# Query pass of linear attention mixed into the GLU stage, sigmoid by tanh, 1/den by head

## The chip, the core and the metric

The kernel runs on one core of one Trainium2 chip. The metric is the device time of one execution in microseconds (us).

Five engines work side by side, each through its own queue in order: TensorE (PE in the profile) multiplies matrices, VectorE (DVE) and ScalarE (ACT) do elementwise work, POOL (GpSimd) does a little of it and hands out most stores, SyncE (SP) hands out most loads and all transposing transfers.

## The reference, cut to what matters

Four residual layers, attention, GLU, attention, GLU, forward and backward in one launch. S = 2048 rows, D = 512, F = 1376, 32 heads of 16. Inputs and outputs are bf16.

```python
def _A_ref(x, wqkv, wo):                       # layers 0 and 2
    ...
    phi = lambda t: jnp.where(t > 0, t + 1, jnp.exp(t)) + 1e-6
    pq, pk = phi(q), phi(k)
    kv = jnp.einsum("bhsd,bhse->bhde", pk, v)
    z = jnp.einsum("bhsd->bhd", pk)
    num = jnp.einsum("bhqd,bhde->bhqe", pq, kv)
    den = jnp.einsum("bhqd,bhd->bhq", pq, z)[..., None] + 1e-6
    o = num / den
    return (... o ...) @ wo

def _B_ref(x, w_gate, w_up, w_down):           # layers 1 and 3
    g = jnp.einsum("bsd,df->bsf", x, w_gate)
    u = jnp.einsum("bsd,df->bsf", x, w_up)
    return jnp.einsum("bsf,fd->bsd", _sigmoid(g) * u, w_down)

x = x + _A_ref(_layernorm(x), A_wqkv, A_wo);  x = x + _B_ref(_layernorm(x), ...)   # twice
# outputs: x and, by jax.vjp, the gradients of x and of all weights
```

An attention layer has two passes. The first takes all keys into a sum (E and z). The second, the **query pass**, needs that sum: queries q, the map phi, the denominator den, the division, the output product y.

## The kernel before

The rows are cut into four blocks of 512 (SB). The parts that the change and the argument touch:

```python
def q_block(k, hT):                            # queries and phi of one block
    for d2 in range(NDC // 2):
        for dc in (2 * d2, 2 * d2 + 1):
            mm4(k, q_ps[:], ...)                                           # TensorE, 4 matmuls
            nc.scalar.activation(eq[:, dc, :], q_ps[:], ACT.Exp)
        nc.vector.tensor_scalar(e2, e2, 1.0, None, ALU.min)                # the clamp
        nc.vector.tensor_scalar(a_t[:], e2, EPS, None, ALU.add)
        for i, dc in ...:
            nc.vector.scalar_tensor_tensor(pq[:, dc, :], qs[i][:], 1.0 + EPS, a_t[:, i, :], ALU.add, ALU.max)
# ... the query pass, after the first pass is over:
    for b in range(NBLK):
        for dc in range(NDC):
            nc.tensor.matmul(d_ps[:], lhsT=Z[:, dc, :], rhs=pe[:, 0, dc, :], ...)   # den, for every channel
            nc.scalar.activation(ld[:], d_ps[:], ACT.Ln, bias=k.eps[:])
            nc.scalar.activation(rd[:], ld[:], ACT.Exp, scale=-1.0)                 # 1/den
            nc.vector.tensor_tensor(qr[:, :, dc, :], pe[:, :, dc, :], rd[:]..., ALU.mult)
        # store qr, turn it (qn) by a transposing transfer, store qn
        if b + 2 < NBLK: qb.append(q_block(k, ln.hT[b + 2]))
        if b: out(b - 1)                       # y of the block before, LayerNorm of the next layer
# ... a unit of the GLU, layers 1 and 3 (eleven a block):
    mm4(k, g_ps[:], ...); mm4(k, u_ps[:], ...)
    nc.scalar.activation(sd[:, 0, :], g_ps[:], ACT.Sigmoid)
    nc.scalar.activation(oms[:], g_ps[:], ACT.Sigmoid, scale=-1.0)
    nc.vector.tensor_tensor(hh[:], u_ps[:], sd[:, 0, :], ALU.mult)
    nc.gpsimd.tensor_tensor(sd[:, 1, :], hh[:], oms[:], ALU.mult)
    # layer 3 also: mm4(dhh_ps), nc.scalar.copy(dhh, ps), dd = dhh * sd on VectorE
```

Weights that layer 3 needs turned (wdT, wuT, wgT) come by transposing transfers on SyncE's queue.

## Time and profile before

1213.13 us, the median of three runs (1212.6 to 1213.26). The trace handed over with it, however, is of another clock. The first experiment profiled the unchanged kernel again, at the timed clock. Columns: span, mean granted clock.

The trace handed over with the kernel before:

```profile
core 0: 1450.6 us, clock 0.749
```

The same kernel profiled again (run e0_before):

```profile
core 0: 1214.3 us, clock 0.969
```

All numbers "before" from here on are of this second trace, except in the prediction, which had only the first.

### The profile page before, as it was taken

Reading aid. Unit: us, or ns where it says so; the run is one execution under the profiler, and the core shown is the slowest. Engines: PE = TensorE matmul, PEld = TensorE weight load, DVE = VectorE, ACT = ScalarE, POOL = GpSimd, SP = SyncE. Lnnn points to the kernel's source line nnn. Section 1 sums busy time; section 2 is a strip of 40 time slices with the busy share of each in tenths; the row PEclk is TensorE's granted clock in tenths of the full one; section 3 lists DMA queues with packets and bytes.
Section 4 is the critical chain, followed back from the end, with each engine's and each line's share of the span. In section 5 each row is a group of like instructions: output and inputs, shape, how many; then the busy total and the mean of one; then the engine's idle time right before and its main releaser. Section 6 shows DMA issues by size and latency. Waiting matters only on the chain.

```text
span 1450.6 us, 14906 instructions
## 1 busy us (share of the span) xinstructions
PE 1392.4 (96%) x5323; PEld 582.4 (40%) x5408; DVE 533.5 (37%) x976; ACT 477.0 (33%) x951; POOL 385.3 (27%) x496
## 2 busy tenths in 40 slices
PE   6989999998999999998999999998999999999997
PEld 3433333443343333333443333443333334533433
DVE  6584333477335243424665344465730000000000
ACT  5475443267514041515336233352440000000000
POOL 4117654104505040402444111143440000000100
PEclk8777777777777777777777777777777777777777
DMA  7978564659915041316847645469539554794651
GB/s 225 226 196 236 196 192 158 145 115 251 256 47 164 26 139 37 104 36 203 297 139 165 210 158 172 162 226 269 176 90 265 130 131 105 174 218 111 154 129 32
DMA packets 355786, 234.47 MB, mean 162 GB/s; under 512 B 279232, under 2 KB 332448, under 8 KB 351616
## 3 DMA queue, kind: packets, MB, share of 16 engines
q1 hardware_dynamic: 336144, 158.24, 44.5%
q0 software_dynamic: 19568, 75.28, 14.3%
q8 instruction: 42, 0.69, 0.2%
q14 instruction: 32, 0.26, 0.1%
HBM read 67.14 MB, written 97.81 MB: 114 GB/s over the span
## 4 chain that ended last, share of the span: by engine, by line
PE 73%; issue 15%; DVE 4%; DMA 4%; POOL 2%; ACT 1%; SPq 1%; another core or an unknown queue 0%; POOLq 0%; DVEq 0%; ACTq 0%
PE dw_ps L996 12%; PE y_ps L162 7%; PE dh_ps L632 7%; PE dh_ps L721 7%; PE g_ps L162 6%; PE u_ps L162 6%; PE dhh_ps L162 6%; PE dh_ps L932 4%; PE q_ps L162 2%; PE dpk_ps L162 2%; PE E_ps L414 2%; PE k_ps L162 2%; PE dh_ps L861 2%; PE dq_ps L162 2%; PE CT_ps L777 2%
## 5 line engine op out<-in xcount | busy, mean ns | idle before, releaser
L996 PE MATMUL dw_ps<-set_t,h_all 128*128 128x512 bf16 (+1 forms) x1008 | 266.6, 439 | 1.7 <-issue 0.2
L996 PEld LDWEIGHTS <-h_all 128*128 128x128 bf16 x1024 | 115.0, 112 | 153.0 <-issue 131.6
L959 ACT CAST dw_new<-dw_ps 128x512 bf16<-128x512 f32 (+2 forms) x51 | 25.2, 578 | 344.7 <-issue 244.0
L960 POOL DMA_DIRECT2D out_dram<-dw_new x51 | 27.4, 542 | 347.9 <-ACT dw_new L959 300.9
L162 PE MATMUL g_ps<-hT_t,wg 128*128 128x512 bf16 x352 | 116.5, 463 | 3.3 <-DMA hT_t<-h_t 2.3
L162 PE MATMUL u_ps<-hT_t,wu 128*128 128x512 bf16 x352 | 116.1, 464 | 0.0
L162 PE MATMUL dhh_ps<-gT_t,wdT 128*128 128x512 bf16 x341 | 113.2, 461 | 0.8
L1010 PE MATMUL dw_ps<-g_all,set_t 128*128 128x512 bf16 (+1 forms) x345 | 99.3, 463 | 0.7
L595 POOL TENSOR_TENSOR sd_t<-hh_t,oms 128x512 bf16<-128x512 bf16 x44 | 51.9, 1180 | 128.6 <-DVE hh_t L594 125.6
L721 PE MATMUL dh_ps<-wgT,dd_t 128*128 128x512 bf16 x174 | 80.4, 462 | 0.9
L721 PE MATMUL dh_ps<-wuT,dd_t 128*128 128x512 bf16 x167 | 77.1, 462 | 1.7 <-DVE dd_t L746 1.6
L162 PEld LDWEIGHTS <-wg 128*128 128x128 bf16 x352 | 39.7, 113 | 63.9 <-issue 63.8
L721 PEld LDWEIGHTS <-dd_t 128*128 128x128 bf16 x352 | 39.7, 113 | 62.0 <-issue 59.0
L1010 PEld LDWEIGHTS <-set_t 128*128 128x128 bf16 (+1 forms) x352 | 40.5, 115 | 59.2 <-issue 55.1
L162 PEld LDWEIGHTS <-wu 128*128 128x128 bf16 x352 | 39.8, 113 | 60.5 <-issue 60.5
L632 PEld LDWEIGHTS <-dd_t 128*128 128x128 bf16 x352 | 39.5, 112 | 60.3 <-issue 60.3
L162 PEld LDWEIGHTS <-wdT 128*128 128x128 bf16 x352 | 39.1, 111 | 60.5 <-issue 60.5
L746 DVE TENSOR_TENSOR dd_t<-dhh_t,sh_t 128x1024 bf16<-128x1024 bf16 x44 | 33.3, 758 | 81.9 <-ACT dhh_t L744 81.9
L785 POOL TENSOR_TENSOR dqT_t<-w_t,qr_l 128x512 bf16<-128x512 bf16 x32 | 38.3, 1208 | 77.3 <-DMA qr_l<-sv_qr_118 39.3
L685 ACT ACTIVATE t_sb<-dh_ps,rstd_132 128x512 f32<-128x512 f32 x16 | 11.0, 687 | 134.8 <-PE dh_ps L632 134.8
L536 POOL TENSOR_TENSOR sd_t<-hhT_t,oms 128x512 bf16<-128x512 bf16 x44 | 51.1, 1177 | 13.9 <-DVE hhT_t L535 9.7
L601 DVE TENSOR_TENSOR dd_t<-dhh_t,sd_t 128x1024 bf16<-128x1024 bf16 x44 | 32.2, 731 | 60.3 <-POOL sd_t L595 59.3
(542 smaller groups left out, 2132.6 us busy)
## 6 DMA issues: line engine op xcount, KB each, us to landing
sv_ddT_123<-dd_t SPq DMA_DIRECT2D x40, 256.0 KB, 2.2
sv_ddT_110<-dd_t SPq DMA_DIRECT2D x40, 256.0 KB, 2.8
sv_sd_112<-sd_t POOLq DMA_DIRECT2D x8, 1024.0 KB, 4.3
sh_t<-sv_sd_112 SPq DMA_DIRECT2D x8, 1024.0 KB, 6.0
out_dram<-dw_new POOLq DMA_DIRECT2D x42, 128.0 KB, 3.6
sv_hhT_109<-hhT_t POOLq DMA_DIRECT2D x4, 1280.0 KB, 6.5
sv_hhT_122<-hh_t POOLq DMA_DIRECT2D x40, 128.0 KB, 2.2
sv_qr_105<-qr_t POOLq DMA_DIRECT2D x4, 1024.0 KB, 5.9
```

Of the source, the lines that this page charges most:

```text
L162: i = k.nc.tensor.matmul(out, lhsT=lhs(c), rhs=rhs(c), start=(c == 0), stop=(c == n - 1))
L414: nc.tensor.matmul(E_ps[ic][:], lhsT=h[:, ic * P:(ic + 1) * P], rhs=pk, start=(st == 0), stop=(st == NST - 1))
L536: pooled(k, nc.gpsimd.tensor_tensor(sd[:, 1, i, :], hhT[:, fc, :], oms[:], ALU.mult))
L595: nc.gpsimd.tensor_tensor(sd[:, 1, :], hh[:], oms[:], ALU.mult)
L601: mul = nc.vector.tensor_tensor(dd[:], dhh[:].unsqueeze(1).to_broadcast([P, 2, SB]), sd[:], ALU.mult)
L632: k.nc.tensor.matmul(dh_ps[:], lhsT=dds[fc][:, a, rows(j)], rhs=(k.wuT, k.wgT)[a][:, fc, :], start=(i == 0), stop=(i == 2 * NFC - 1))
L721: nc.tensor.matmul(acc[b][j][:], lhsT=dd[:, a, rows(j)], rhs=(k.wuT, k.wgT)[a][:, fc, :], start=(fc == 0 and a == 0), stop=(fc == NFC - 1 ...
L746: nc.vector.tensor_tensor(dd[:], dhh[:].unsqueeze(1).to_broadcast([P, 2, SB]), sh[:, :, i, :], ALU.mult)
L785: nc.gpsimd.tensor_tensor(dqT[:, dc, :], w_t[:], rp[:, dc, :], ALU.mult)
L932: nc.tensor.matmul(dh[j][:], lhsT=lhs(j, c), rhs=rhs(c), start=False, stop=stop and c == NDC - 1)
L996: k.nc.tensor.matmul(ps[ic][:, 0:w], lhsT=h_t[:, ic * P:(ic + 1) * P], rhs=t, start=(i == 0 and st == 0), stop=(i == len(srcs) - 1 and st ...
L1010: k.nc.tensor.matmul(p[0:r, :], lhsT=t[:, f:f + r], rhs=g_t, start=(i == 0 and st == 0), stop=(i == len(srcs) - 1 and st == NST - 1))
```

## The change

Its intent: let TensorE do GLU matmuls while VectorE and ScalarE catch up with the query pass. For that the query pass becomes a generator that hands out small units, half of them before the GLU starts, half among its units. Mixing the two would switch ScalarE's function tables all the time, so sigmoid becomes 0.5(1 - tanh(-g/2)) out of the table that has exp. The Trainium skill ("ScalarE: Activation LUTs", Table sets: the hidden batching unit) lists exp and tanh in one set; the trace has four table loads before (1.28 us each). That table names ln only in another set, and run g2 below, which takes Ln and Exp back while keeping tanh, has five table loads. So 1/den is taken by head: 64 short matmuls, a reciprocal, a mask, and 16 matmuls that spread it over the channels. One clamp per pair goes to POOL.

```diff
@@ forward @@
-            a_fwd(k, 0, lns[0], lns[1])
-            b_fwd(k, 1, lns[1], lns[2])
+        second = A0.second(lns[1])
+        next(second)                                  # the half before the GLU
+        for b, fc in b_fwd(k, 1, lns[1], lns[2]):
+            next(second, None)                        # one unit after each GLU unit
+            if b == NBLK - 1 and fc in (4, 6, 8, 10):
+                A2.keys((fc - 4) // 2)
         ... the same for layers 2 and 3, two units per GLU unit of block 0;
         ... wuT and wgT are asked for when the query pass is used up (before: at units 0 and 4)
@@ query @@
-        nc.vector.tensor_scalar(e2, e2, 1.0, None, ALU.min)
-        nc.vector.tensor_scalar(a_t[:], e2, EPS, None, ALU.add)
+        nc.vector.tensor_scalar(a_t[:], pe[:, 1], 1.0, EPS, ALU.min, ALU.add)
+        nc.gpsimd.tensor_scalar(pe[:, 1], pe[:, 1], 1.0, None, ALU.min)
@@ den and share @@
-            nc.tensor.matmul(d_ps[:], lhsT=Z[:, dc, :], rhs=pe[:, 0, dc, :], ...)
-            nc.scalar.activation(ld[:], d_ps[:], ACT.Ln, bias=k.eps[:])
-            nc.scalar.activation(rd[:], ld[:], ACT.Exp, scale=-1.0)
+        for j in range(NB):
+            for dc in range(NDC):
+                nc.tensor.matmul(d_ps[32 * j:32 * j + 32, :], lhsT=self.Z[:, dc, :],
+                                 rhs=self.pe[b, dc // 2][:, 0, dc % 2, rows(j)], ...)
+        nc.scalar.activation(d_t[:], d_ps[:], ACT.Identity, bias=k.eps[:])
+        nc.vector.reciprocal(d_t[:], d_t[:])
+        nc.vector.tensor_tensor(self.RD[b][:], d_t[:]..., k.tmask[:]..., ALU.mult)
+            nc.tensor.matmul(ps[:], lhsT=k.spread[:, 2 * d2 + i, :], rhs=self.RD[b][:]..., ...)
+            nc.scalar.copy(rd[:, i, :], ps[:])
@@ second, layer 2 @@
+            k.wdT = k.p_wa.tile([P, NDC, F], BF16, name="wdT", tag="wkvo")   # in the place of wk, wv, wo
+            nc.sync.dma_start_transpose(out=k.wdT[:], in_=k.w_in["wd"])      # so only when these are used up
@@ glu @@
-    nc.scalar.activation(sd[:, 0, i, :], g_ps[:], ACT.Sigmoid)
-    nc.scalar.activation(oms[:], g_ps[:], ACT.Sigmoid, scale=-1.0)
+    nc.scalar.activation(th[:], g_ps[:], ACT.Tanh, scale=-0.5)
+    nc.scalar.activation(sd[:, 0, :], th[:], ACT.Identity, bias=k.onef[:], scale=-1.0)
+    nc.scalar.activation(sd[:, 1, :], th[:], ACT.Identity, bias=k.onef[:])
```

Cut from this diff: buffers (six shared ones for queries and keys in place of pools of two), saving MT and kv to memory for the backward, a few forced orders at the start, and wdT's reload in the backward.

## The prediction

> **What bounds it now.** The page's busy table has TensorE busy 1392 of 1450.6 us (96%); VectorE 37%, ScalarE 33%, POOL 27%. But this execution fell in a slow state: the clock record holds 0.752 from 25 us on with only one core running. The Trainium skill ("TensorE: Matmul & The Clock Gate", the limiter note in Part 1) says one or two busy cores never trip the limiter; this trace disagrees. The timed runs (1213 us) must have had a higher clock. The timeline shows back-to-back 512-column matmuls every 284 ns; by that page's N/2.4+2.5 they take 216 ns at full clock. About 4900 such matmuls (counted from the source) give an estimate of 1058 us, so in timed runs some 90 to 155 us are not TensorE: more than the 58 us idle shown here. What is TensorE-bound in the trace can be bound by the other engines when timed.
>
> **Where that idle time lies.** The table of 10 us stretches: in attention's second pass (60 to 110 us and 298 to 350 us) VectorE is busy 8 to 9 and ScalarE up to 9.5 of each 10 us. Per layer I sum VectorE at about 50 us (q 16 x 0.69, clamps 16 x 0.43, q/den 16 x 0.69, residual 16 x 0.69, LN, copies), ScalarE 34 to 40 (Exp 0.60, Ln 0.69, Exp(-ln) 0.63, copies 0.59), against TensorE 160 matmuls = 45 us here, 35 us at full clock. So about 15 us per attention layer are lost when timed. Smaller losses: start (11.5 us in the first 20); 2.6 us at 36 us (key pool of two, waiting on key transposes); 2.3 us before layer 3's first g (hidden state's transpose); 4.4 us at 662 us (chain: wqkv's transpose 6.8, then qr load 5.3).
>
> **What the change does.**
> - Half of each second pass runs among GLU matmuls, the rest before them: the prefix still has about 33 us of VectorE work against 25 us of TensorE. I expect 8 to 10 us back per layer.
> - Ln+Exp (1.31 us x 16 per layer) becomes a 0.59 us copy; three of four table loads (1.28 us each) go; one clamp per pair goes to POOL.
> - TensorE gains 16 spreading matmuls per layer and 64 short den matmuls for 16 long: 4 to 4.5 us per layer, on the critical path.
> - GLU on ScalarE: two sigmoids (1.19) become tanh and two affine passes (estimate 1.9 from the Ln and Exp forms). With the dhh copy that is 2.5 us per unit against 2.6 us of TensorE: nearly critical in layer 3, with slack in down and dh.
> - Six key/query buffers and keys taken early: 4 to 6 us. Instruction order: qr's load now precedes wqkv's transpose: 3 to 4 us.
> - Costs: wuT/wgT requested at the tenth unit instead of the first and fifth; they took 20 us in the trace, needed after about 17: 2 us. wdT's transpose (10.5 us) stands before layer 3's first hidden transposes: 0 to 5 us. MT reloaded: 1 us.
>
> **Sum:** about -33 + 9 = -24 us.
>
> Predicted 1189 us, 80% range 1168 to 1210. Chances: faster over 2% 0.50, same 0.46, slower 0.04.
>
> **Shown right if** the second pass has no stretches with TensorE below 9 of 10 once GLU matmuls start; only one table load remains; rd matmuls cost about 3.5 us per layer; layer 3's unit pitch stays at twelve matmuls. **Wrong if** ScalarE exceeds TensorE in the GLU units (TensorE waiting on a g or u bank), if the gap before layer 3's first g grows, or if dh waits for wuT.
>
> **What would make it wrong:** a timed clock below full, which shrinks the idle time to be won while the added matmuls stay; ScalarE's three passes being slower; POOL's clamp and VectorE holding each other up.

## More of the kernel before

The instruction groups of VectorE in layer 0's query pass (busy us, mean ns of one | idle time before them):

```profile
L336 DVE SCALAR_TENSOR_TENSOR pe_t<-q_ps,a_t 128x512 bf16<-128x512 f32 x16 | 10.4, 684 | 0.1
L473 DVE TENSOR_TENSOR qr_t<-pe_t,rd_t 128x1024 bf16<-128x1024 bf16 x15 | 10.0, 686 | 1.4 <-ACT rd_t L472 1.3
...
L334 DVE TENSOR_SCALAR a_t<-pe_t 128x1024 bf16<-128x1024 bf16 x8 | 3.6, 450 | 0.1
L333 DVE TENSOR_SCALAR pe_t<-pe_t 128x1024 bf16<-128x1024 bf16 x8 | 3.4, 421 | 0.8 <-ACT pe_t L329 0.8
```

L333 is the clamp: 0.42 us each, 3.4 us a layer. That is what the change moves to POOL.

The view by windows gives, for a stretch of time, its length and each engine's busy time (number of instructions in brackets). I chose four stretches: the two query passes alone (layers 0 and 2, each from the last matmul of the first pass to the first GLU matmul), and the query pass together with the GLU layer that follows (up to the last product with w_down for layers 0 and 1; up to the last forward matmul for layers 2 and 3).

```profile
core 0: us, PE busy (x) PEld busy (x) DVE busy (x) ACT busy (x) POOL busy (x), PEclk, DMA share, GB/s
55.90:98.70 42.80, 35.77 (x187) 15.80 (x184) 38.39 (x83) 34.02 (x61) 8.20 (x15) 0.96 0.84 214
260.20:306.30 46.10, 36.15 (x187) 15.88 (x184) 40.67 (x89) 36.98 (x68) 8.77 (x16) 0.96 0.74 188
...
55.90:224.90 169.00, 156.26 (x731) 69.16 (x727) 99.57 (x198) 102.07 (x203) 96.18 (x131) 0.98 0.76 229
260.20:547.80 287.60, 269.68 (x1251) 120.62 (x1248) 152.33 (x273) 133.50 (x267) 102.57 (x137) 0.98 0.54 145
```

Read it so: in layer 0's query pass TensorE works 35.8 of 42.8 us and is idle 7.0; in layer 2's it is idle 10.0. So 17 us is all of TensorE's idle time that there is to win in the two query passes. VectorE is busy 38.4 of the 42.8 us (90%): it is nearer its limit than TensorE (84%), and POOL is nearly free. In the longer stretches TensorE is idle 12.7 and 17.9 us.

TensorE's timeline shows where it waits: the bracket at a line's end is the idle time just before it and what ended it. Three of its waits in layer 3 and at the start of the backward:

```profile
306.33 0.59 PE L162 MATMUL g_ps<-hT_t,wg 128*128 128x512 bf16 x1 [3.03 <-DMA hT_t<-h_t]
...
346.45 1.86 PE L162 MATMUL g_ps<-hT_t,wg 128*128 128x512 bf16 x4 [7.92 <-DVE hh_t L594]
...
563.63 0.61 PE L782 MATMUL t_ps<-u_t,bdmask 128*128 128x512 bf16 x1 [7.62 <-DVE u_t L817]
```

The last two have nothing to do with the query pass.

## The result, and the profile after

The changed kernel is right and takes 1244.98 us, the median of four runs (1242.17 to 1248.96); the kernel before in the same rounds took 1213.2 (1212.6 to 1213.55). The ratio is 1.0265, 95% interval 1.0236 to 1.0294: slower by 2.65%, where I had predicted 1189 us, faster. Ratios here and below are the mean time of one kernel's fast runs over that of the other's of the same rounds, so not quite the ratio of the medians that are quoted.

The two traces, cut at the last forward matmul: the forward grew from 547.8 to 578.1 us (+30.3), the backward shrank by 4.1. The same two long stretches as before, by windows:

```profile
core 0: us, PE busy (x) PEld busy (x) DVE busy (x) ACT busy (x) POOL busy (x), PEclk, DMA share, GB/s
56.30:243.20 186.90, 164.23 (x806) 72.25 (x803) 111.43 (x200) 124.38 (x238) 134.39 (x169) 0.95 0.75 214
272.50:578.10 305.60, 272.32 (x1319) 122.07 (x1316) 157.29 (x269) 153.95 (x303) 128.68 (x151) 0.96 0.54 146
```

TensorE's idle time in them was to go. It grew, from 12.7 to 22.7 us and from 17.9 to 33.3 us. Its busy time grew too, by 8.0 and 2.6 us (some of that are keys of layer 2 that are now taken in layer 1). VectorE, which was to be relieved, has 11.9 and 5.0 us more; POOL has 38 and 26 us more.

TensorE's timeline has four large waits that the kernel before does not have:

```profile
130.03 1.86 PE L179 MATMUL u_ps<-hT_t,wu 128*128 128x512 bf16 x4 [6.83 <-ACT rd_t L475]
...
313.95 0.26 PE L458 MATMUL den_ps<-pe_t,Z_t 128*32 128x128 bf16 x1 [11.50 <-DVE pe_t L450]
322.50 0.61 PE L179 MATMUL g_ps<-hT_t,wg 128*128 128x512 bf16 x1 [8.29 <-DMA hT_t<-h_t]
...
394.60 1.86 PE L704 MATMUL dh_ps<-wgT,sd_t 128*128 128x512 bf16 x4 [4.57 <-DMA wgT<-in_B_w_gate_dram]
```

The second and third answer to the 3.03 us wait before (layer 3's first GLU matmul). Follow them back. POOL's timeline just before:

```profile
296.03 0.23 POOL L255 TENSOR_SCALAR ln_neg<-x_sum 128x2 f32<-128x2 f32 x1
306.23 0.64 POOL L379 DMA_DIRECT2D sv_qn_125<-qn_t  x1 [9.97 <-DMA qn_t<-pe_t]
306.95 0.18 POOL L261 TENSOR_SCALAR rstd_140<-ln_ss 128x2 f32<-128x2 f32 x1
```

POOL stood for 10 us at a store (of the turned queries, qn) whose data had not landed, and LayerNorm's tiny rstd stood behind it. The SyncE queue tells why the data was late: wdT's transpose takes 8.8 us of the queue, then the two transposes of qn 5.7, and the last hidden state (hT) that the GLU needs comes after the gradient's transpose of 5.7 us.

```profile
289.64 8.83 SPq L557 DMA_TRANSPOSE wdT<-in_B_w_down_dram  x1
298.52 5.73 SPq L480 DMA_TRANSPOSE qn_t<-pe_t  x2
...
308.86 5.70 SPq L644 DMA_TRANSPOSE gT_t<-in_grad_out_dram  x1
314.66 2.03 SPq L266 DMA_TRANSPOSE hT_t<-h_t  x1
```

VectorE, in order too, waits 7.7 us for that rstd, with the residual and the next queries behind it:

```profile
308.72 1.28 DVE L264 TENSOR_SCALAR h_t<-x_90,ln_neg,rstd_140 128x512 bf16<-128x512 f32 x1 [7.68 <-POOL rstd_140 L262]
```

The wait at 130 us has the same form: POOL's in-order queue of clamps (2.8 us each), products and stores delays ln_neg, ScalarE stands at the LayerNorm instruction behind it, and 1/den's copy (rd) stands behind that:

```profile
126.76 0.72 ACT L259 ACTIVATE ln_junk<-x_96,ln_neg 128x512 bf16<-128x512 f32 x1 [7.25 <-POOL ln_neg L255]
```

The Trainium skill ("PSUM — Partial Sum Buffer", Engine vs sequencer instructions) says that the queues of ScalarE, VectorE and GpSimd (POOL) "are strict FIFO"; these lines are what that looks like when two stages share them.

Last, the GLU's three ScalarE passes, whole program (before: two Sigmoids of 0.60 us each, 1.19 us a unit):

```profile
L602 ACT ACTIVATE sd_t<-th_t,onef 128x512 bf16<-128x512 f32 x88 | 63.4, 721 | 3.2
L604 ACT ACTIVATE sd_t<-th_t,onef 128x512 bf16<-128x512 f32 x88 | 62.3, 708 | 0.0
L601 ACT ACTIVATE th_t<-g_ps 128x512 f32<-128x512 f32 x88 | 51.3, 587 | 15.6 <-PE g_ps L179 14.8
```

2.02 us a unit, near the 1.9 that I had estimated.

After this reading I had two theories: Q, three waits behind queues (behind wdT's transpose, behind the clamp on POOL, behind wuT and wgT) are the loss; S, ScalarE's third pass is. Later runs forced a third, V: the new 1/den and the clamp on POOL cost what they cost, whether mixed or not.

### The profile page after: what moved, and what is told of

It reads as the page before. It is cut to its first block, busy times and chain, and to the rows that moved or that the text cites. A ratio compares the mean times of both kernels' runs of the same rounds, so it can differ in the third digit from the quotient of the medians.

```text
span 1240.5 us, 15505 instructions
## 1 busy us (share of the span) xinstructions
PE 1109.0 (89%) x5536; PEld 511.5 (41%) x5536; DVE 548.4 (44%) x968; ACT 513.2 (41%) x1020; POOL 454.0 (37%) x563
## 5 line engine op out<-in xcount | busy, mean ns | idle before, releaser
L1070 PE MATMUL dw_ps<-set_t,h_all 128*128 128x512 bf16 (+1 forms) x1024 | 207.3, 366 | 3.1 <-DMA set_t<-sv_ddT_116 3.1
L1070 PEld LDWEIGHTS <-h_all 128*128 128x128 bf16 x1024 | 100.9, 99 | 109.3 <-issue 7.2
L605 POOL TENSOR_TENSOR sd_t<-sd_t,hh_t 128x512 bf16<-128x512 bf16 x88 | 105.6, 1200 | 105.5 <-ACT sd_t L604 45.0
L179 PE MATMUL g_ps<-hT_t,wg 128*128 128x512 bf16 x352 | 93.6, 389 | 12.3 <-DMA hT_t<-h_t 11.5
L179 PE MATMUL u_ps<-hT_t,wu 128*128 128x512 bf16 x352 | 92.8, 387 | 7.7 <-ACT rd_t L475 7.4
L179 PE MATMUL dhh_ps<-gT_t,wdT 128*128 128x512 bf16 x352 | 89.8, 379 | 0.0
L179 PE MATMUL y_ps<-wd,hh_t 128*128 128x512 bf16 x352 | 78.0, 379 | 2.0 <-DVE hh_t L603 2.0
L603 DVE SCALAR_TENSOR_TENSOR hh_t<-sd_t,u_ps 128x512 bf16<-128x512 bf16 x88 | 60.1, 683 | 25.3 <-ACT sd_t L602 23.4
L602 ACT ACTIVATE sd_t<-th_t,onef 128x512 bf16<-128x512 f32 x88 | 63.4, 721 | 3.2
L604 ACT ACTIVATE sd_t<-th_t,onef 128x512 bf16<-128x512 f32 x88 | 62.3, 708 | 0.0
L601 ACT ACTIVATE th_t<-g_ps 128x512 f32<-128x512 f32 x88 | 51.3, 587 | 15.6 <-PE g_ps L179 14.8
L676 DVE TENSOR_TENSOR sd_t<-dhh_t,sd_t 128x1024 bf16<-128x1024 bf16 x44 | 33.4, 761 | 51.1 <-POOL sd_t L605 51.1
L815 DVE TENSOR_TENSOR dd_t<-dhh_t,sh_t 128x1024 bf16<-128x1024 bf16 x44 | 32.1, 737 | 53.2 <-ACT dhh_t L813 47.9
L704 PEld LDWEIGHTS <-sd_t 128*128 128x128 bf16 x352 | 34.6, 99 | 49.2 <-issue 8.7
```

Of the source, the lines that this page charges most:

```text
L179: i = k.nc.tensor.matmul(out, lhsT=lhs(c), rhs=rhs(c), start=(c == 0), stop=(c == n - 1))
L601: nc.scalar.activation(th[:], g_ps[:], ACT.Tanh, scale=-0.5)
L602: nc.scalar.activation(sd[:, 0, :], th[:], ACT.Identity, bias=k.onef[:], scale=-1.0)
L603: nc.vector.scalar_tensor_tensor(hh[:], sd[:, 0, :], 0.5, u_ps[:], ALU.mult, ALU.mult)
L604: nc.scalar.activation(sd[:, 1, :], th[:], ACT.Identity, bias=k.onef[:])
L605: pooled(k, nc.gpsimd.tensor_tensor(sd[:, 1, :], sd[:, 1, :], hh[:], ALU.mult))
```

## The experiments

### One wait at a time

First the kernel before alone, for its trace.

> The kernel before, unchanged, to get its trace at the full clock (the first trace fell at 0.75). Theory Q (queues: the changed kernel's loss is three waits, behind wdT's transpose on SP, behind the clamp on POOL, behind wuT/wgT): at full clock TensorE idle in the first 440 us of the kernel before is well under the 76 us of the changed kernel, and no single wait of TensorE at the entry of layer 3 is over 5 us. Theory S (ScalarE: the GLU's third pass holds TensorE): the kernel before is ahead mostly inside its GLU blocks (unit pitch 1.73 us in layer 1 against a longer one after), not at the stage borders.

Measured: 1216.04 us, one profiled run at clock 0.969. Its lines are shown above. In the first 440 us TensorE is idle 51.2 us, in the changed kernel 75.6, and no wait at layer 3's entry is over 5 us: as theory Q had it.

Then three edits to the changed kernel, each taking one suspect away. The last two give wrong results (the weight isn't turned).

```diff
 e1_clamp_dve
-        nc.gpsimd.tensor_scalar(pe[:, 1], pe[:, 1], 1.0, None, ALU.min)
+        nc.vector.tensor_scalar(pe[:, 1], pe[:, 1], 1.0, None, ALU.min)
 e2_wdT_plain
-            nc.sync.dma_start_transpose(out=k.wdT[:], in_=k.w_in["wd"])
+            nc.sync.dma_start(out=flat(k.wdT), in_=k.w_in["wd"]...)        # same bytes, not turned
 e3_wuwg_plain: the same for wuT and wgT
```

> The clamp of exp(q) back from POOL (2.8 us each, 16 of them) to VectorE (estimate 0.43 us each). Theory Q: the 6.8 us wait of TensorE at 123 us and part of the waits at 80 to 100 us go; 8 to 15 us faster than the changed kernel, about 1230 to 1237 us, ratio to before 1.014 to 1.02. Theory S: no gain, plus up to 3 us for VectorE, about 1245 us.

Measured: 1246.85 us, ratio to before 1.028 (1.0244 to 1.0316). No gain. The wait at 130 us fell to 2.0 us, but at layer 3's entry the pair only changed from 11.5 and 8.3 us to 7.8 and 10.7.

> wrong result on purpose: layer 3's wdT comes by a plain DMA of the same bytes instead of a transposing one, so the SP queue is not held 8.8 us. Theory Q: the 20 us wait at 303 to 322 us shrinks to under 6; 14 to 19 us faster than the changed kernel, about 1226 to 1231 us. Theory S: under 3 us.

Measured: 1240.67 us, 1.0229 (1.0192 to 1.0267). About a quarter of what Q expected, and the interval overlaps that of the changed kernel: the pair became 7.1 and 4.0 us, the 130 us wait grew to 7.4. The qn transposes now took 10 us of the queue by themselves.

> wrong result on purpose: wuT and wgT by plain DMAs of the same bytes. Theory Q: the waits of 1.7 and 4.6 us at 386 and 390 us go; 5 to 7 us faster than the changed kernel, about 1238 us. Theory S: no change, 1245 us.

Measured: 1242.5 us, 1.0238 (1.0197 to 1.0278): about 2.5 us of the 5 to 7 expected, not clear of the noise.

So each suspect is real in the trace and worth little in time: take it away and the next one in the same queue binds. Two more edits went at the cause of layer 3's entry, one at mixing, one at theory S.

```diff
 f1_qn_later: the store of qn is handed out two LayerNorm or GLU steps later
-            self.turned.append((self.sv["qn"][b], self.qn[b]))
-            self.store_turned()
+            store_later(k, 2, out=self.sv["qn"][b], in_=flat(self.qn[b]))      # but for the last block
 f2_entry3: f1, and wdT is turned in layer 1, in four slices, into scratch memory
+            if b == 2 and fc in (3, 5, 7, 9):
+                nc.sync.dma_start_transpose(out=t[:], in_=k.w_in["wd"][:, c * P:(c + 1) * P])
+                store_later(k, 2, out=k.wdT_d[c], in_=t[:])
-            nc.sync.dma_start_transpose(out=k.wdT[:], in_=k.w_in["wd"])
+            nc.sync.dma_start(out=k.wdT[:], in_=k.wdT_d[:]...)
   and the next block's gradient is ordered behind the hidden state
 f3_no_mix: mixing undone
-        next(second)
+        for _ in second: pass                                                   # both attention layers
 f4_two_pass: wrong result on purpose, the third ScalarE pass left out
-    nc.scalar.activation(sd[:, 1, :], th[:], ACT.Identity, bias=k.onef[:])
```

> The kernel after with one thing moved: the stores of the turned queries are handed out two LayerNorm or GLU steps later, so that POOL's in-order queue no longer waits for the transposes (10 us in the kernel after, before layer 3's first GLU matmul) ahead of LayerNorm's rstd. Theory Q1 (the program order of POOL's stores is the cause): TensorE's two waits of 11.5 and 8.3 us at layer 3's entry shrink together to 10 us or less, total 1232 to 1236 us. Theory Q2 (the DMA burst is: weight transpose, turned queries, gradient and hidden state all in the same 25 us): the first wait shrinks, the second one takes most of it back, total within 4 us of 1245. Theory S (ScalarE's third pass): no change.

Measured: 1242.08 us (1234.97 to 1250.44), 1.0243 (1.0183 to 1.0303). The 11.5 us wait is gone and the one for the hidden state grew from 8.3 to 15.3 us: what Q2 expected.

> As the run before, and wdT is no longer transposed at layer 3's entry: four slices are transposed during layer 1 into scratch memory and loaded plainly; block 1's gradient cannot be asked for before block 0's hidden state is turned. The result stays right. If the entry's queues are the cause of layer 3's late start (Q1 and Q2 together), the two waits fall from 20 us to 6 or less and the total is 1226 to 1231 us. If they only move to another place (VectorE's work, the clamp), it stays above 1238.

Measured: 1238.65 us, 1.021 (1.015 to 1.0269). The 11.5 us wait is gone from the trace and POOL's 10 us stand too, but the hidden state's wait stays as long as it was, and a wait near 130 us is still there:

```profile
126.99 1.86 PE L180 MATMUL y_ps<-M_t,pe_t 128*128 128x512 bf16 x4 [4.34 <-ACT rd_t L482]
...
313.38 1.89 PE L180 MATMUL g_ps<-hT_t,wg 128*128 128x512 bf16 x4 [8.49 <-DMA hT_t<-h_t]
```

Layer 3's entry came 9 us earlier than in the changed kernel and the forward ended only 6 us earlier. Mending the order of the queues is worth about half a per cent at most: the interval overlaps that of the changed kernel.

> Wrong result on purpose: the GLU's third ScalarE pass (0.71 us per unit, 88 units) is left out, the product takes the second pass's output. Theory S (ScalarE holds the GLU stages): 10 us or more faster than after, 1235 or less. Theory Q (queues at the stage borders): ScalarE is not what TensorE waits for in a unit, so at most 4 us.

Measured: 1243.18 us, 1.0263 (1.0221 to 1.0304), against 1.0265 for the changed kernel. Theory S falls.

### Mixing undone

> The kernel after with the mixing alone undone: each query pass is finished before the first GLU unit, all else stays. My prediction gave mixing 8 to 10 us per attention layer: then this is 16 to 20 us slower than after, near 1262. If the second pass was bound by TensorE at full clock already (before had only 7 and 10 us of TensorE idle there), mixing wins little, and what it costs in waits at layer 3's entry comes off: 1230 to 1245.

Measured: 1244.15 us, 1.0278 (1.0229 to 1.0327). Not 16 to 20 us slower: no difference from the mixed kernel. But this run had a flaw. With the query pass over early, wuT and wgT were asked for at the first GLU unit, their transposes stood ahead of block 1's hidden state, and TensorE waited 11.0 us there. The flaw was mended in a later run, which asks for them at the tenth unit as the changed kernel does:

```diff
 h4_nomix_late: f3, and
-                if next(second, None) is None and actx:
+                if fc == 9:
```

> The kernel after without mixing again, mended: in the first such run the up and gate weights' transposes came seven units earlier than in after and stood ahead of block 1's hidden state in the queue, an 11 us wait of TensorE that mixing has nothing to do with. Here they are asked for at the tenth unit, as in after. If that wait was all that made mixing look neutral, this takes 1232 to 1237, and mixing costs 8 us or more. If mixing is worth what I predicted (16 to 20 us), it stays above 1255.

Measured: 1242.73 us (five runs), 1.0246 (1.0211 to 1.028). The changed kernel has 1.0265 (1.0236 to 1.0294). Mixing is worth nothing measurable here, in either direction. The stretches by windows, to be held against those of the changed kernel:

```profile
58.00:244.10 186.10, 161.44 (x797) 71.97 (x804) 108.07 (x200) 123.59 (x238) 133.23 (x169) 0.96 0.74 214
275.20:574.20 299.00, 272.16 (x1293) 122.25 (x1315) 156.51 (x269) 153.95 (x303) 129.49 (x151) 0.97 0.56 149
```

TensorE is idle 24.7 and 26.8 us, mixed 22.7 and 33.3. In these two traces, one of each kernel, mixing has 2 us less in the first pair of layers and 6.5 more in the second. And the loss against before is there without it: in its query passes TensorE waits for VectorE's products,

```profile
97.00 0.26 PE L459 MATMUL den_ps<-pe_t,Z_t 128*32 128x128 bf16 x1 [5.13 <-DVE pe_t L451]
...
315.83 0.26 PE L459 MATMUL den_ps<-pe_t,Z_t 128*32 128x128 bf16 x1 [8.88 <-DVE pe_t L451]
```

### Undoing the query pass's parts, without mixing

These two were made from f3 (with its flaw, so f3 is what they compare with). g3 puts all mends of the queues and the clamp's return into the mixed kernel. g4 is explained below.

```diff
 g1_nomix_clamp: f3 and e1 together
 g2_nomix_ln: g1, and 1/den as in the kernel before
+        self.table = nc.scalar.preload_act_table_set("natural_log_exp_and_others")
-            nc.tensor.matmul(ps[:], lhsT=k.spread[:, 2 * d2 + i, :], rhs=self.RD[b][:]..., ...)
-            nc.scalar.copy(rd[:, i, :], ps[:])
+            nc.tensor.matmul(ps[:], lhsT=self.Z[:, 2 * d2 + i, :], rhs=pe[:, 0, i, :], ...)
+            nc.scalar.activation(ld[:], ps[:], ACT.Ln, bias=k.eps[:])
+            nc.scalar.activation(rd[:, i, :], ld[:], ACT.Exp, scale=-1.0)
   (den, reciprocal and mask removed)
 g3_combo: f2 and e1 together
```

> Mixing undone (as in the run before, 1244 us) and the clamp back on VectorE. In the run without mixing VectorE holds the query pass: the matmuls of den wait 5.9 and 8.9 us for its products while POOL's clamps (22.5 us in that pass) slow some of its instructions (h_t 987 ns in place of 544). Theory V (VectorE is what the second pass is short of, and the clamp on POOL gave none of it back because both engines slow each other): 4 to 10 us faster than without mixing, 1234 to 1240. Rival (the den chain's length, not VectorE's load): within 3 us of 1244.

Measured: 1239.85 us, 1.0204 (1.017 to 1.0239), 0.7% below f3, or 4.3 us: at the lower end of what theory V expected.

> As the run just above, and 1/den goes back to the way of the kernel before: four 512-column matmuls with the wide Z, ScalarE's Ln and Exp(-ln), no reciprocal, no spread; two table loads per layer come back. If the new 1/den (two VectorE passes of 0.95 and 0.75 us and 16 more matmuls on a chain that every head waits for) is what lengthens the query pass from 43 to 59 us, this takes 10 to 14 us per layer off the forward: 1212 to 1222. If buffers, the third ScalarE pass or the late weights are at fault instead, it stays above 1230.

Measured: 1232.75 us (1232.45 to 1233.86), 1.015 (1.0126 to 1.0174). A gain again, of 7 us, but the expectation was 18 us or more, and the result stays above 1230, where it put the case that buffers, the third ScalarE pass or the late weights are at fault. 1.5% stay over before, in a kernel that has neither the mixing nor the clamp on POOL nor the new 1/den. In them are a 12.5 us wait for the hidden state, the flaw of f3, where before has 7.9 us, and waits of y for the divided queries (2.8, 4.1, 3.8 and 6.1 us in layer 0's pass) that before does not have. A likely reason for the latter is the order of the units, made for mixing, in which the output follows the division at once and not a block later. No run isolates that.

> The mixed kernel with all mends of its queues: turned queries stored later, wdT turned in layer 1, next gradient held back, clamp on VectorE. Result right. If the losses are only waits of queues, 1222 to 1230. If the extra VectorE and TensorE work of the new 1/den stays as the cause, 1233 to 1240.

Measured: 1246.78 us (1236.45 to 1253.47), 1.0256 (1.0196 to 1.0317). Worse than either theory expected, with a wide spread. So in the mixed kernel all four mends together bring nothing that shows above this spread.

### One part alone, added to the kernel before

Undoing parts in a kernel whose waits replace each other cannot size them. So I added them to the kernel before, one by one.

```diff
 h1_before_den: before, with 1/den by head (Z of 32 columns, 64 den matmuls, reciprocal, mask,
                spreading matmuls and copies as in the change; den of block b right after its queries)
 h2_before_clamp: before, with
-        nc.vector.tensor_scalar(e2, e2, 1.0, None, ALU.min)
-        nc.vector.tensor_scalar(a_t[:], e2, EPS, None, ALU.add)
+        nc.vector.tensor_scalar(a_t[:], e2, 1.0, EPS, ALU.min, ALU.add)
+        nc.gpsimd.tensor_scalar(e2, e2, 1.0, None, ALU.min)
 h3_before_tanh: before, with the GLU by tanh and two affine passes, dhh scaled by 0.5
```

> The kernel before with one part of the change alone: 1/den by head (64 short matmuls per layer, reciprocal, masked spread, 16 spreading matmuls, ScalarE copies). Worked out from durations: TensorE +4.8 us per layer, VectorE +6.8 us, ScalarE -11 us. If VectorE (38.4 busy of 42.8 us in that pass of before) is what the pass is short of, it grows by 5 to 9 us per layer: 1223 to 1231. If ScalarE's Ln and Exp were holding it, as my prediction had it, no slower than before: 1205 to 1215.

Measured: 1237.39 us against 1213.14, ratio 1.0193 (1.0157 to 1.0228). Layer 0's query pass by windows, and the new VectorE groups in it:

```profile
57.10:110.30 53.20, 42.74 (x257) 19.09 (x258) 46.05 (x96) 25.69 (x50) 8.29 (x15) 0.90 0.70 180
```

```profile
L486 DVE RECIPROCAL d_t<-d_t 128x128 f32<-128x128 f32 x4 | 3.8, 951 | 3.6 <-ACT d_t L485 3.5
...
L488 DVE TENSOR_TENSOR RD_t<-d_t,tmask 128x512 bf16<-128x512 f32 x4 | 2.7, 681 | 0.1
```

The pass grew from 42.8 to 53.2 us. VectorE has 7.7 us more (6.5 of it in these two groups), TensorE 7.0 us more; ScalarE has 8.3 us less, which helps nothing. Of TensorE's 7.0 us some 4.2 are den and spreading (3.9 and 5.1 us, against 4.8 for den before). In layer 2 the pass grew from 46.1 to 61.8 us; 8.6 of these are a wait for the hidden state at layer 3's first GLU matmul, which is 3.0 us in before. The reciprocal takes 0.95 us for 128 columns, longer than the 0.68 us for 512 columns of an ordinary pass. The Trainium skill ("VectorE: DVE Perf Modes", First, the fixed hardware budget) says that reciprocal is an iterated divide with a repeat count of 8; the trace agrees in direction.

> The kernel before with the clamp alone moved to POOL. By the sums of busy time it takes 3.4 us of VectorE per layer away: 1207 to 1210. If POOL's 2.8 us clamp and VectorE slow each other, as the no-mix runs suggest, nothing or a loss: 1212 to 1220.

Measured: 1226.52 us against 1213.14, ratio 1.0111 (1.0074 to 1.0147). Moving 3.4 us a layer from the busiest elementwise engine to an idle one costs 1.1%, more than the upper end of what even the rival expected. Layer 0's query pass by windows, then groups of POOL and VectorE in it:

```profile
54.50:105.80 51.30, 36.09 (x182) 16.37 (x181) 40.96 (x78) 34.41 (x64) 30.69 (x24) 0.87 0.63 179
```

```profile
L334 POOL TENSOR_SCALAR pe_t<-pe_t 128x1024 bf16<-128x1024 bf16 x8 | 22.1, 2775 | 1.6 <-DVE a_t L333 1.4
```

```profile
L473 DVE TENSOR_TENSOR qr_t<-pe_t,rd_t 128x1024 bf16<-128x1024 bf16 x14 | 12.6, 913 | 7.8 <-POOL pe_t L334 4.5 <-ACT rd_t L472 3.2
L336 DVE SCALAR_TENSOR_TENSOR pe_t<-q_ps,a_t 128x512 bf16<-128x512 f32 x16 | 10.3, 683 | 0.2
...
L333 DVE TENSOR_SCALAR a_t<-pe_t 128x1024 bf16<-128x1024 bf16 x8 | 5.0, 624 | 0.3
```

Three things are to be seen. The clamp takes POOL 2.78 us where VectorE took 0.42. The division (qr_t) waits 4.5 us for it. And VectorE's own instructions became longer while POOL works: the division from 686 to 913 ns, a_t from 450 to 624, so that VectorE's busy time did not fall (38.4 before, 41.0 now). The pass that reads PSUM (L336) did not change, 684 and 683. The Trainium skill ("SBUF — State Buffer", Who interferes with whom) says that VectorE's two-port modes, and its passes with two SBUF inputs, share a port pair with POOL, that the pair is locked for a whole instruction, and that the loser "fully blocks". The direction and the kinds of instruction agree. Over both layers most instructions kept their length and a few took far longer, as blocking would have it: the division has a median of 692 ns (before 685) and a longest of 1900 (before 693), a_t a median of 427 (before 426) and a longest of 1761 (before 642). The equal medians also show that the second operation that a_t now does is not what lengthens it. The division by the view of tiles (shortest, median and longest in ns), before and with the clamp on POOL:

```profile
L473 DVE TENSOR_TENSOR qr_t<-pe_t,rd_t x32: 680/685/693, 66.3 to 303.7; 128x1024 bf16<-128x1024 bf16 x32
L473 DVE TENSOR_TENSOR qr_t<-pe_t,rd_t x32: 677/692/1900, 65.3 to 315.6; 128x1024 bf16<-128x1024 bf16 x32
```

> The kernel before with the GLU alone changed: tanh and two affine passes (2.0 us of ScalarE a unit in place of 1.2). My prediction had this near critical only in layer 3. If ScalarE is off the path: 1212 to 1216. If layer 1's units (8 matmuls, 1.73 us of TensorE) are now held by ScalarE's 2.0 us: 4 to 8 us slower, 1217 to 1222.

Measured: 1208.4 us against 1213.14, ratio 0.9949 (0.9913 to 0.9984). The three-pass GLU alone costs nothing; it was a little faster. The trace shows where: the 7.92 us wait of before in layer 3 has become 1.75 us.

```profile
346.97 7.51 PE L164 MATMUL y_ps<-wd,hh_t 128*128 128x512 bf16 x33 [1.75 <-DVE hh_t L599]
```

In before POOL stood 8.5 us at its clearing of wuT's last rows, until their transpose had landed, with GLU products behind it. Here the clearing ran at the same moment (344.0 us, before 343.4) but stood later in POOL's order, behind nine GLU products of layer 3 and not seven, so POOL waited only 4.5 us for it. So I read this gain as one of order, not of tanh; the best version below agrees.

The three parts alone add up to 1.93% + 1.11% - 0.51% = 2.53%, and the whole change costs 2.65%. In microseconds of before that is an estimate of +23, +13 and -6. So close a match is partly luck: the change also holds gains and losses that are in none of the three (4.1 us won in the backward, the waits for wuT and wgT, the order of the units), and g2 is still 1.5% slower without two of the parts.

### Is it only VectorE and POOL, then?

> Wrong result on purpose: the mixed kernel with its queues mended (as f2, 1239 us), and in addition no clamp at all and no reciprocal and masked spread on VectorE (ScalarE writes den straight into the tile; den and spreading matmuls, copies and all order stay). It asks what mixing is worth when VectorE and POOL aren't loaded by the change. If the clamp and VectorE's part of 1/den are what eats the gain: 1205 to 1218, 20 to 33 us off f2. If the waits come from the mixed order itself (queues, buffers, order on engines): above 1228.

```diff
 i1_cheap_mix: f2, and (wrong result on purpose)
-        nc.gpsimd.tensor_scalar(pe[:, 1], pe[:, 1], 1.0, None, ALU.min)
-        nc.vector.reciprocal(d_t[:], d_t[:])
-        nc.vector.tensor_tensor(self.RD[b][:], d_t[:]..., k.tmask[:]..., ALU.mult)
+        nc.gpsimd.memset(self.RD[b][:, 1:NB, :], 0.0)
+        nc.scalar.activation(self.RD[b][:, 0, :], d_ps[:], ACT.Identity, bias=k.eps[:])
```

Measured: 1239.98 us, 1.023 (1.0197 to 1.0263); f2 had 1.021. Nothing was won: the second case of the expectation. In the stretch from 58 to 244 us VectorE's busy time is 100.9 us (f2: 109.6) and POOL's 114.4 (f2: 136.2), but the waits of the queues are as long as ever. The chain at 129 us, on POOL, on ScalarE and on TensorE:

```profile
123.52 0.59 POOL L201 DMA_DIRECT2D sv_qn<-qn_t  x1 [6.95 <-issue]
```

```profile
126.66 0.72 ACT L260 ACTIVATE ln_junk<-x,ln_neg 128x512 bf16<-128x512 f32 x1 [8.68 <-POOL ln_neg L256]
```

```profile
94.08 1.86 PE L180 MATMUL g_ps<-hT_t,wg 128*128 128x512 bf16 x4 [9.78 <-DMA hT_t<-h_t]
...
129.31 1.86 PE L180 MATMUL y_ps<-M_t,pe_t 128*128 128x512 bf16 x4 [7.54 <-ACT rd_t L478]
```

For the store's own 6.95 us the profile names no cause. Part of this is of the run's own making: the turned slices of wdT that f2 added stand in the same SyncE queue just there. But it shows that the mixed order has a second reason to be slow, which hides behind the first: a store or a transpose of one stage, at the head of a queue that both stages use, holds both. A mixed kernel with queues free of this was not found; whether mixing could pay in one stays open.

### A version that beats both

The lines of before showed two waits that the query pass has no part in. g4 mends these, i2 adds the tanh GLU.

```diff
 g4_before_plus
-    nc.gpsimd.memset(t[0:FDUP, NFC - 1, :], 0.0)          # right behind the transposes of wuT, wgT
+                if b == 1 and fc == 1:                     # a block later, after a product on POOL
+                    for t in (k.wuT, k.wgT):
+                        after(k, nc.gpsimd.memset(t[0:FDUP, NFC - 1, :], 0.0), prod)
-            if b == 0 and l == 2:                          # backward: wo and wqkv turned ahead of qr's use
-                nc.sync.dma_start_transpose(...); nc.sync.dma_start_transpose(...)
+                if b == 0 and dc == 0 and l == 2:          # held until the first product with qr is done
+                    held(k, u, nc.sync.dma_start_transpose(...), nc.sync.dma_start_transpose(...))
 i2_best: g4 and h3 together
```

> The kernel before with two mends that its own full-speed trace asks for: POOL's clearing of the last rows of wuT and wgT no longer waits (8.5 us) for their transposes ahead of GLU products (TensorE's wait of 7.9 us in layer 3 behind it), and the backward's first load of saved queries goes ahead of the transpose of wqkv (TensorE's wait of 7.6 us). Expected 8 to 13 us faster than before, 1200 to 1206, if the waits aren't taken over by the next.

Measured: 1206.16 us against 1214.65, ratio 0.9913 (0.9875 to 0.9951).

> What the single-part runs point to: the kernel before with the part of the change that paid (tanh GLU, 1208 alone) and the two mends of g4 (1206 alone); no mixing, clamp on VectorE, Ln and Exp kept. If the two gains add: 1199 to 1203. But the tanh GLU and the later clearing both act on the same wait of layer 3 (7.9 us in before, 1.75 us in the tanh run), so part of it counts twice: 1200 to 1206 is what I expect.

Measured: 1202.57 us against 1214.52, ratio 0.9909 (0.9874 to 0.9944), with a right result. It beats both kernels, before by 0.9% (a small gain, but the interval leaves out 1) and, through before, the changed one by an estimated 3.5% (0.9909 / 1.0265). As g4 has 0.9913 without tanh, the gain of h3 does not add: it was the same wait of layer 3.

## Why the prediction was wrong

The sum in the prediction was "about -33 + 9 = -24 us". It came out at +32.

**The step that failed first: "So about 15 us per attention layer are lost when timed", and from it "I expect 8 to 10 us back per layer".** I had only a trace at clock 0.75 and scaled: 50 us of VectorE work against 35 us of TensorE. The trace at full clock has 42.8 and 46.1 us for the two passes, with 38.4 and 40.7 us of VectorE and 7.0 and 10.0 us of TensorE idle. The work that I summed to 50 us is there, but part of it ran beside GLU matmuls already: in layer 0 six of the 16 residual passes and 12 of the 16 that write LayerNorm's h come after the first GLU matmul. So nearly half of the 30 us that I held to be lost was not there. The total I had right: 90 to 155 us not TensorE, and the page has 1105 of 1214 us busy, so 109 (the spacing of 216 ns that it took for matmuls of 512 columns is what the trace at full clock shows: eleven take 2.54 us, of which the last has 0.38). I had put it in the wrong place: about half of it is in the backward. What was left to win, mixing did not win either: undone, with the weights asked for at the same point, the kernel takes 1.0246 of before, mixed 1.0265. So the largest term of the sum, 16 to 20 us for two layers, came out as nothing measurable, with VectorE's waits replaced by those of shared queues.

**The step that was left out: what the rewriting costs VectorE.** The prediction lists "TensorE gains 16 spreading matmuls per layer and 64 short den matmuls for 16 long: 4 to 4.5 us per layer" and books Ln and Exp as a saving on ScalarE. It says nothing of reciprocal and mask, 6.5 us of VectorE a layer, on the engine that I had just named as the busy one. TensorE's term was sized well (4.2 us in h1); what it left out was larger. Alone, 1/den by head costs 1.9%, some 12 us a layer.

**"One clamp per pair goes to POOL" was booked as a gain; it costs 1.1%.** The risk stood in the text ("POOL's clamp and VectorE holding each other up"), but I had not priced the clamp on POOL. It takes 2.78 us, 6.6 times VectorE's time.

**"Six key/query buffers and keys taken early: 4 to 6 us": not seen.** Layer 0's first pass ends at 56.3 us, before at 55.9.

**"wdT's transpose stands before layer 3's first hidden transposes: 0 to 5 us" was the right place and too small.** The wait at layer 3's first GLU matmul went from 3.0 to 8.3 us, and an 11.5 us wait came ahead of it. But e2, f1 and f2 show that mending it returns about half a per cent at most and not the sum of the waits. The estimate for wuT and wgT, 2 us, was small too: TensorE waited 4.6 us for wgT (e3 won about 2.5, within the noise).

**Right:** one table load left; the GLU's pass estimate (1.9, measured 2.02) and that it costs little; the backward ("3 to 4 us", measured 4.1 for the whole backward: the wait of 7.62 us for the first saved queries became 1.15). The three named signs of being wrong were good ones: the gap before layer 3's first g did grow, and dh did wait for wgT; TensorE waiting on a bank because of ScalarE's passes was not the cause, as f4 shows.

What is shown and what is not: the costs of the three parts are measured alone, on the kernel before. That mixing wins nothing measurable is shown on the changed kernel, by h4. That the three costs add up inside the changed kernel is not shown, though their sum meets the whole. There, undoing the clamp and 1/den without mixing returned 0.7% and 0.5% and left 1.5%. That rest may be waits that took the place of those undone, or a cost of the rewriting that no run isolates: the order of the units, the shared buffers, the late weights. Its cause stays open.

## What to carry to other kernels

Before planning to fill an engine's idle time, measure that idle time at the clock at which the kernel is timed, in the very stage, and list what the rewriting adds to the engine that is nearest its limit there. Moving work to an idle engine is a gain only if that engine does it about as fast and does not slow the first. When two stages are mixed they share every in-order queue: look for stores and transfers that wait for data ahead of small instructions that the other stage needs, and if taking one such wait away changes nothing, size the parts by adding each alone to the old kernel.

## What the Trainium skill lacked or had wrong

- "TensorE: Matmul & The Clock Gate", Part 1, lacks a state. Its limiter note says that one or two busy cores never trip the limiter, and speaks of a clock of 13/16 (0.81). The first trace, one core alone, has 0.75 from 25 us on and a mean of 0.749 over 1450.6 us, so it is not that limiter's clock and does not speak against the note; the same kernel had 0.969 and 1214.3 us at another time. The cause is not known from these runs.
- "GPSIMD Engine Reference", Engine selection, calls one-input elementwise work on POOL "roughly line-rate" against VectorE. Here the one-input clamp over 128x1024 bf16 took 2775 ns on POOL and 421 ns on VectorE (spans on POOL are rough in the profile, but the division that needs it waited for it).
- "SBUF — State Buffer", Who interferes with whom: these runs agree with it; it gives ratios of slowed instructions, but no share of instructions that are hit in a mixed stream. With the clamp on POOL, VectorE's two-input pass went from 686 to 913 ns on average and the one-input pass from 450 to 624 (medians unchanged, the longest 1900 and 1761), while the pass reading PSUM stayed at 684 and 683.
- "VectorE: DVE Perf Modes" says that reciprocal is iterated; I found no page that gives its duration. Here it took 941 to 955 ns for 128x128 f32.
- "PSUM — Partial Sum Buffer" says that queues are strict FIFO. I found no page that warns of what follows for stores issued by POOL: one store that waited for its data held a LayerNorm instruction of 0.18 us, and all behind it, for 9.97 us.
